# One table of numbers: the order of all steps, and the engines and queues of the movable ones, in a fused mLSTM and gated MLP kernel

## The chip, the cores and the metric

The kernel runs on one core of one Trainium2 chip, in one launch. The metric is the device time in microseconds; lower is better. The engines are named as in the profile: PE is TensorE (its weight loads are PEld), DVE is VectorE, ACT is ScalarE, POOL is GpSimd, SP is SyncE, which here only issues DMAs.

## The reference

The first half is a gated linear recurrence over 768 positions, for 4 batches and 8 heads of width 40; the second a gated MLP whose gate mixes positions.

```python
# q, k, v, o_gate: (4, 8, 768, 40); i_gate, f_gate: (4, 8, 768)
for t in range(S):
    m_new = np.maximum(f_gate[:, :, t] + m, i_gate[:, :, t])
    f_stab = np.exp(f_gate[:, :, t] + m - m_new)
    i_stab = np.exp(i_gate[:, :, t] - m_new)
    m = m_new
    C = f_stab[:, :, None, None] * C + i_stab[:, :, None, None] * np.einsum('bhd,bhe->bhde', vt, kt)
    n = f_stab[:, :, None] * n + i_stab[:, :, None] * kt
    h_tilde = np.einsum('bhde,bhe->bhd', C, qt)
    denom = np.maximum(np.abs(np.einsum('bhd,bhd->bh', n, qt)[:, :, None]), 1.0)
    y[:, :, t] = h_tilde / denom / (1.0 + np.exp(-o_gate[:, :, t]))
x = y.transpose(0, 2, 1, 3).reshape(B, S, H * D)        # (4, 768, 320)
h = np.maximum(x @ w_in, 0.0)                            # w_in (320, 1024)
u, v = h[..., :512], h[..., 512:]
v_n = (v - mean(v)) / np.sqrt(var(v) + 1e-06)
v_s = np.einsum('ts,bsd->btd', w_spatial, v_n) + b_spatial[None, :, None]
return (u * v_s) @ w_out                                 # w_out (512, 320)
```

## The kernel before

**Steps.** The program is a list of some 1,590 named steps. A step is a few instructions of one engine, or one DMA. It has a list of the engines that may run it, a few dependences, and a place in the table `ORDER` (lines 49 to 104). Nothing else sets the order: `ordered()` (line 162) reads the table from left to right, and the program emits the steps in that order. So the table gives each engine its queue, and each DMA queue (the one that SP issues, the one that ACT issues) its order. A name may carry a suffix: `:V`, `:A`, `:P`, `:S` puts the step on DVE, ACT, POOL or SP; without one it goes to the first engine of its list. The table also hands out the buffers: a tile takes the first free slot of its pool (`POOLS`, line 36) when its first step is reached, and gives it back behind its last step.

```python
    for t in order:
        for b in t.bufs:
            if b.slot is None:
                b.slot = open_[b.pool].pop(0)
            used[b] = used.get(b, 0) + 1
            if used[b] == b.users:
                open_[b.pool].append(b.slot)
```

So a load that is moved can land in another slot, and then waits for another tile's last reader. Pool QK (3 slots) holds the q and k of a chunk and, early on, the raw halves of w_in.

**The attention half.** The recurrence is done in 24 chunks n of 128 positions (6 for each batch, in the order of the batches), each of two halves of 64. First the gates are turned into the exponents g and a, in three pieces z of the sequence: positions 0 to 127, 128 to 383, 384 to 767 (`PIECES`). For piece z: loads f and i; on DVE or POOL the scan m, then fa, fs, the scan g, is, as; then gh, gl and ah, al, which split g and a into a high and a low float. Piece 0 of batch 0 goes directly into the tiles GM0 and AT0 (dg0 to dg3, da). The rest makes a round trip through DRAM: wg and wa write g and a (tiles gp and ap) to scratch (scr_g, scr_a; lines 391 and 395), gm (line 500) and ra (line 414) read them back as rows of the tiles GM and AT. ra01 and ra02 read pieces 1 and 2 of a for batch 0. Chunk 0 needs piece 0, chunks 1 and 2 piece 1, chunks 3 to 5 piece 2.

For chunk n on PE: s (line 518, 32 matmuls 64 columns wide: the scores), ex (line 521, one matmul 512 wide of AT and GM: the exponents), for batch 0 ebm (line 530, 512 wide), dc (lines 557 and 559, 16 matmuls: what the chunk adds to the state), pv (lines 585 and 586, 16 matmuls: the chunk's output), px (lines 618 and 619, three transposes of the output). Between them on ACT, DVE and POOL: W and Eb (exponentials of ex and ebm), ks (scores times W), q and kt (scaled q and k), d1, c1, d2, c2 (the state, from chunk to chunk), th (tanh of the output gate), den, xm, xg (the division and the gate), xh, xj, xl, xk (high and low halves of the transposed output).

**The MLP half.** Every fp32 product is three matmuls, of high and low halves (H·H, H·L, L·H). The weights are loaded raw and split: wi1j and wi0j for w_in (halves v and u, three row blocks j), ws for w_spatial, wo for w_out; of each _ld is the load (512 KB for one of w_in), _t, _b, _l are on DVE, _x on ACT, _h on either. For batch b, block k of 128 positions: V{b}{k} on PE (line 659, 8 matmuls 512 wide, x times w_in's half for v), then re, sq, va, po, nb, vn, vh, vl (relu, normalisation, split). pu (line 701) gives u. pb{b}{hf}{d}{s} (lines 711 to 713) mixes the positions, then g, gu, gh, gl; c (lines 734 to 736) multiplies by w_out, oc copies, out stores. The MLP steps of one batch stand among the attention steps of the next, so PE has both kinds until the last batch.

Of the kernel before, what the change touches and what calls it, by code (L numbers as in the profile page):

```python
# [49 lines left out]
mk1 i0 f0:A m0 rst0 ident ksz2 f1 rst1 rh0_1:A i1 fa0 qk0:A fs0 is0 wi10_ld ws02_ld g0 m1 as0 f2 gh0:V ah0 fa1 wi10_x al0 cg0 fs1 gl0 mk0 cg1 ca0 g1 ey0 gh1 i2:S wi12_ld  # L50
is1:P m2 wa0 rhz0 dg2 dg0:A as1 wi10_t da dg1 wi12_t ws02_h gl1 s0 dg3 wi00_ld:A ex0 rh0_0 fa2 ah1 fs2 ksz0:V g2 qz wg1 ksz1 cz0 al1:P wi10_b wa1 W0 wg0 wi12_x kt0:V rhz1
ebm0 ks0_1 wi11_ld wi00_t gm2 ra01 gm1 dc0 Eb0 rh1_1:A wi10_h eg21 is2:P q0_1 ks0_0 wi00_x as2:P th0 wi12_b c1_0 qk1 wi01_ld:A rhz2 gh2 eg00 pv0 ex1 wi12_h ey1 gl2:P
wi00_b wi10_l ah2 ws02_l:P wg2 ebm1 rh1_0:A wi11_t ebm2 wi12_l ex2 wi11_x wi02_ld:A Eb1 den0 wi11_b W1 xm0 al2:P d2_0:P xg0 kt1 wi11_h wi01_x wi01_t px0 c2_0 s1 rh2_1
qk2:A xj0:V xh0 wi11_l ws11_ld:A d1_1:P wa2 xl0 xk0 ks1_1 gm4:A q1_0 dc1 wi02_x ws12_ld wi01_b wi02_t Eb2 c1_1 q1_1 d2_1:P V00 rh2_0 wi01_h W2 q2_0 ks1_0 th1 gm3 wi00_h
wi02_b ra02 wi01_l pv1 q2_1 s2 rh3_0:A rh3_1:A ex3 c2_1 wi00_l den1 re00 qk3 xm1 ebm3 th2 sq00 kt2 ebm4 ks2_0 dc2 xg1 d1_2:P ks2_1 c1_2 s3 d2_2:P Eb3 px1 ex4 gm5:A W3
wi02_h Eb4 kt3 pv2 q3_1:V eg10 c2_2 xh1 ws01_ld:A qk4 ks3_0 d1_3:P ks3_1 th3 dc3 s4 q3_0 W4 den2 xm2 xg2 c1_3 eg20 xj1 qk5 s5 rh4_1 rh5_1:A eg11 xk1 pv3 d2_3 rh4_0 eg01
xl1 wo1_ld c2_3 ebm5 wi02_l ca1 Eb5 px2 rh5_0 ex5 xj2 ws00_ld:A den3 va00 xk2 ra12 W5 kt4 xm3 xh2 dc4 q4_0 V01 d1_4:P gm6 ks4_0 xl2 xg3 ws11_h ks4_1 px3 q5_1 c1_4 ws01_h
# [746 lines left out]
```

## Time and profile before

| | |
|---|---|
| three runs | 366.48, 367.25, 368.3 us (median 367.25) |
| the profiled execution, its own time | 365.34 us |
| its span, first to last instruction | 363.6 us |
| PE busy | 337.6 us, 93% of the span |
| DVE, ACT, POOL busy | 258.7, 126.9, 111.0 us |
| moved by DMA | 39.46 MB, 109 GB/s over the span |
| mean granted clock of TensorE | 0.972 |

The page cuts the span into 40 slices (9.1 us each), so slice 5 begins at 36 us. The granted clock is the share of TensorE's full speed that the throttle gave. A stretch (a view of the trace from one time to another) gives each engine's busy time within it, in the order PE, PEld, DVE, ACT, POOL, then the clock, the DMA engines' mean busy share and what they moved. The timeline gives one row for each instruction, with its start and length, and in brackets what it waited for. The chain of waits is followed back from the last instruction.

### The profile page before, as it was taken

To read this page: it belongs to the slowest core of one execution; us is meant where nothing else is said; L and a number is where in the kernel's file an instruction comes from. 1 tells how busy PE (TensorE), PEld (TensorE's weight loads), DVE (VectorE), ACT (ScalarE), POOL (GpSimd) and SP (SyncE) were. 2 spreads that over 40 slices of the span, in tenths; PEclk is the share of its full clock that TensorE was granted. 3 is DMA by queue.
4 is the path that set the end of the run, shared out by engine and by line. 5 is a ranking of instruction groups with operands and counts; after the bars stand their busy time and mean duration, and the time that the engine had idled before them with its cause. 6 is when DMAs were issued, how large, how long until landed. Compare 5 with 4: busy or idle time off the path is not lost.

```text
span 363.6 us, 9097 instructions
## 1 busy us (share of the span) xinstructions
PE 337.6 (93%) x3654; PEld 309.7 (85%) x3654; DVE 258.7 (71%) x590; ACT 126.9 (35%) x302; POOL 111.0 (31%) x133
## 2 busy tenths in 40 slices
PE   0378899999999899999999999999999999999995
PEld 0246697889999898999999988899999988999995
DVE  3989477997978848976498579766958686728152
ACT  1384426582324025272022253540310235432021
POOL 6475664686134241423100003332230231100000
PEclk9999657999999999999999999999999999999999
DMA  7489963843444770143405150443042300001002
GB/s 227 153 229 293 227 177 118 240 150 101 131 139 119 192 191 10 58 140 110 113 31 138 53 153 6 116 117 105 22 127 69 117 2 19 2 0 38 18 20 73
DMA packets 17218, 39.46 MB, mean 109 GB/s; under 512 B 4012, under 2 KB 7660, under 8 KB 17176
## 3 DMA queue, kind: packets, MB, share of 16 engines
q1 hardware_dynamic: 9540, 20.85, 20.7%
q10 hardware_dynamic: 7476, 17.92, 16.9%
q8 instruction: 29, 0.48, 0.6%
q0 software_dynamic: 160, 0.11, 0.1%
q14 instruction: 13, 0.11, 0.1%
HBM read 34.43 MB, written 4.42 MB: 107 GB/s over the span
## 4 chain that ended last, share of the span: by engine, by line
PE 79%; DMA 9%; DVE 6%; ACT 2%; issue 1%; SPq 1%; POOL 0%; DVEq 0%
PE pm L659 11%; PE pu L701 11%; PE pb L711 10%; PE pb L713 9%; PE pb L712 9%; PE s L518 5%; PE pv L585 4%; PE pc L734 4%; PE pc L736 3%; PE pc L735 3%; PE dc L557 3%; PE ex L521 2%; DMA AT<-scr_a 2%; DMA QK<-in_qk 2%; DMA scr_a<-ap 2%; PE px L618 2%
## 5 line engine op out<-in xcount | busy, mean ns | idle before, releaser
L711 PE MATMUL pb<-wsH,vH 128*128 128x384 f32 x192 | 66.5, 346 | 0.2 <-DVE vL L250 0.2
L713 PE MATMUL pb<-wsH,vL 128*128 128x384 f32 x192 | 64.8, 338 | 0.0
L712 PE MATMUL pb<-wsL,vH 128*128 128x384 f32 x192 | 64.8, 338 | 0.0
L250 POOL TENSOR_TENSOR KS<-QK,Eb 40x512 f32<-40x512 f32 x33 | 43.1, 1309 | 28.0 <-DMA Eb<-scr_e 18.1
L518 PE MATMUL s<-QK 40*64 40x64 f32 x768 | 30.3, 240 | 12.5 <-DMA QK<-in_qk 12.5
L518 PEld LDWEIGHTS s<-QK 40*64 40x64 f32 x768 | 27.7, 153 | 14.6 <-DMA QK<-in_qk 9.9
L711 PEld LDWEIGHTS pb<-wsH,vH 128*128 128x128 f32 x192 | 36.1, 188 | 1.4 <-DVE vL L250 0.5
L712 PEld LDWEIGHTS pb<-wsL,vH 128*128 128x128 f32 x192 | 36.1, 188 | 0.7
L671 POOL TENSOR_TENSOR st<-st,half_neg 128x1 f32<-128x1 f32 x24 | 13.5, 569 | 74.6 <-DVE st L669 63.9
L713 PEld LDWEIGHTS pb<-wsH,vL 128*128 128x128 f32 x192 | 36.0, 188 | 0.0
L250 DVE TENSOR_TENSOR pb<-pb,bsp 128x384 f32<-128x384 f32 x32 | 17.7, 561 | 24.3 <-PE pb L713 24.3
L250 DVE TENSOR_TENSOR KS<-s,W 64x512 f32<-64x512 f32 x48 | 32.7, 687 | 1.6 <-PE s L518 0.6
L701 PE MATMUL pu<-xH,wiH 128*128 128x384 f32 x96 | 32.6, 340 | 0.0
L701 PE MATMUL pu<-xH,wiL 128*128 128x384 f32 x96 | 32.4, 337 | 0.0
L734 PE MATMUL pc<-woH,gt 128*128 128x320 f32 x96 | 30.9, 322 | 0.0
L659 PE MATMUL pm<-wiH,xH 128*128 128x512 f32 x72 | 30.7, 426 | 0.2
L585 PEld LDWEIGHTS pv<-RH,KS 104*64 104x64 f32 x384 | 26.1, 148 | 5.2 <-issue 2.4
L533 ACT ACTIVATE W<-ex 128x512 f32<-128x512 f32 x24 | 14.3, 597 | 44.7 <-PE ex L521 35.0
L736 PE MATMUL pc<-woH,gt 128*128 128x320 f32 x96 | 29.8, 310 | 0.0
L585 PE MATMUL pv<-RH,KS 104*64 104x41 f32 x384 | 28.4, 240 | 1.4 <-DVE KS L250 0.9
L735 PE MATMUL pc<-woL,gt 128*128 128x320 f32 x96 | 29.6, 308 | 0.0
L659 PE MATMUL pm<-wiL,xH 128*128 128x512 f32 x72 | 29.1, 405 | 0.0
(159 smaller groups left out, 769.3 us busy)
## 6 DMA issues: line engine op xcount, KB each, us to landing
QK<-in_qk SPq DMA_DIRECT2D x15, 448.0 KB
RH<-in_vk ACTq DMA_DIRECT2D x24, 256.0 KB
RH<-in_vk SPq DMA_DIRECT2D x24, 256.0 KB
QK<-in_qk ACTq DMA_DIRECT2D x9, 448.0 KB
out<-o ACTq DMA_DIRECT2D x14, 160.0 KB
Eb<-scr_e SPq DMA_DIRECT2D x22, 80.0 KB
out<-o SPq DMA_DIRECT2D x10, 160.0 KB
wir<-in_w_in SPq DMA_DIRECT2D x3, 512.0 KB
```

Of the source, the lines that this page charges most:

```text
L250: return lambda e: e.tensor_tensor(out=out(), in0=in0(), in1=in1(), op=op)
L518: self.nc.tensor.matmul(o[64 - p0:128 - p0, h], q[p0:p0 + D, 0, h], q[p0:p0 + D, 1, h], start=True, stop=True)
L533: job(f"W{n}", act(512), lambda e: e.activation(out=self.T(W), in_=ext(), func=AF.Exp), r=[ex], w=[W], due=D0 + 1)
L585: self.nc.tensor.matmul(o[0:64, h], ks[0:ke, 0, h], v0[0:ke, h], start=True, stop=True)
L659: self.nc.tensor.matmul(pmt(), l, r, start=i == 0, stop=i == len(terms) - 1)
L701: self.nc.tensor.matmul(put(), w, x, start=i == 0, stop=i == len(terms) - 1)
L711: self.nc.tensor.matmul(pbt(), vH[:, cd], wh[:, s], start=s == 0, stop=False)
L712: self.nc.tensor.matmul(pbt(), vH[:, cd], wl[:, s], start=False, stop=False)
L713: self.nc.tensor.matmul(pbt(), vL[:, cd], wh[:, s], start=False, stop=s == NB - 1)
L734: self.nc.tensor.matmul(pct(), gH[:, c], wh[:, d], start=d == 0, stop=False)
L735: self.nc.tensor.matmul(pct(), gH[:, c], wl[:, d], start=False, stop=False)
L736: self.nc.tensor.matmul(pct(), gL[:, c], wh[:, d], start=False, stop=d == 3)
```

## The change

Only the table is another one. The diff is 54 lines of the table against 55, all of them different (later line numbers are one higher); one line of either:

```diff
 ORDER = """
...
-qk2:A xj0:V xh0 wi11_l ws11_ld:A d1_1:P wa2 xl0 xk0 ks1_1 gm4:A q1_0 dc1 wi02_x ws12_ld wi01_b wi02_t Eb2 c1_1 q1_1 d2_1:P V00 rh2_0 wi01_h W2 q2_0 ks1_0 th1 gm3 wi00_h
...
+ra11 d2_0:P s1 qk2 wa2:A c2_0 den0 ksz2 eg20 wi01_h q1_0 xm0 kt1 qk3:A wi02_x dc1 d1_1:P ey1 Eb2 xg0 ra02 px0 ex2 ebm3 ks1_1 c1_1 d2_1:P xh0 ks1_0 xj0 pv1 ws02_ld xk0
...
 """
```

The same steps stand in both tables. On other engines than before are: 59 DMAs that ACT issued and SP now issues, 49 the other way; 45 steps from DVE to ACT, 49 from ACT to DVE; 31 from DVE to POOL, 32 from POOL to DVE. PE's steps have one engine only; their order is another. In the first batch, from ex3 on, PE has

- before: ex3 ebm3 ebm4 dc2 s3 px1 ex4 pv2 dc3 s4 s5 pv3 ebm5 px2 ex5 dc4 V01 px3 V02
- after: ex3 s2 dc2 px1 s3 pv2 dc3 ebm4 s4 pv3 ex4 ebm5 px2 V01 ex5 px3 dc4 s5 V02

and ebm3 and pv1 stand ahead of ex3 in the second. The set of PE steps ahead of V02 is the same in both. Of PE's rows of narrow steps (s, dc, pv, ex, ebm, px, with no step of the MLP between them) the one between V00 and V01 is by far the longest in both orders; behind V02 none of either order sums to more than 3.6 us at full clock.

PE, just ahead of V01 (its tile is pm01). Before, V01 stands behind px2, ex5 and the 16 matmuls of dc4, of which the first is shown:

```order
L530 MATMUL eb5_654<-GM1_74,AT0_73 128x512
L618 MATMUL px2_660<-ident_71,x2_601 128x128 x2
L619 MATMUL px2_660<-ident_71,x2_601 64x128
L521 MATMUL ex5_665<-GM1_74,AT0_73 128x512
L557 MATMUL dc4_682<-RH1_80 40x41
```

In the changed kernel, the same place on PE, ahead of V01:

```order
L522 MATMUL ex4_627<-GM0_72,AT0_73 128x512
L531 MATMUL eb5_632<-GM1_74,AT0_73 128x512
L619 MATMUL px2_636<-ident_71,x2_603 128x128 x2
L620 MATMUL px2_636<-ident_71,x2_603 64x128
L660 MATMUL pm01_641<-wiH_83,xH00_389 128x512
```

V01 now directly follows px2; ex5, px3, dc4 and s5 stand between V01 and V02.

The queue of SP before, around wa2 (scr_a from ap2) and ra02 (AT0 from scr_a, 384 wide); RH2 from in_vk are the halves of chunk 2's v and k, wsr12 a third of half of w_spatial:

```order
L391 DMA scr_g_57<-gp2_257 32x12x64
L478 DMA RH2_81<-in_vk 64x1024
L395 DMA scr_a_59<-ap2_284 64x1x384
L453 DMA wsr12_382<-in_w_sp 128x768
L478 DMA RH2_81<-in_vk 64x1024
L500 DMA GM1_74<-scr_g_57 4x512
L414 DMA AT0_73<-scr_a_59 16x384
```

ACT in the changed kernel, around wa2; Eb1 and W1 are exponentials of chunk 1, ap2 by CAST is ah2, the step on RH0 is th0. Eight instructions ahead of this piece on ACT stands ra01 (AT0 from scr_a, 256 wide):

```order
L533 ACTIVATE Eb1_273<-eb1_266 128x512
L255 CAST ap2_279<-it_96 32x384
L396 DMA scr_a_59<-ap0_157 64x1x128
L479 DMA RH2_81<-in_vk 64x1024
L534 ACTIVATE W1_310<-ex1_286 128x512
L548 ACTIVATE RH0_79<-RH0_79 128x320
L396 DMA scr_a_59<-ap2_279 64x1x384
```

wa2 has moved from SP to ACT and stands there behind W1 and th0; ra02 is still issued by SP (behind qk2's load), ra01 by ACT instead of SP, and wa1 by SP in both (now behind the load of wi01).

## Rows read from the trace of the kernel before

**Rows 1.** The page: busy time of each engine, and TensorE's granted clock by slice.

```profile
PE 337.6 (93%) x3654; PEld 309.7 (85%) x3654; DVE 258.7 (71%) x590; ACT 126.9 (35%) x302; POOL 111.0 (31%) x133
...
PEclk9999657999999999999999999999999999999999
```

**Rows 2.** Stretches: from:to, us, busy PE PEld DVE ACT POOL, clock, DMA share, GB/s.

```profile
4.30:17.40 13.10, 2.27 (x33) 2.08 (x33) 11.01 (x24) 3.56 (x7) 6.94 (x12) 1.00 0.72 212
33.50:39.06 5.56, 2.31 (x65) 2.11 (x65) 4.74 (x12) 3.35 (x9) 2.77 (x3) 1.00 1.04 238
39.06:56.34 17.28, 17.28 (x269) 14.33 (x269) 10.02 (x24) 6.28 (x17) 10.49 (x13) 0.50 0.75 185
62.00:120.00 58.00, 57.96 (x736) 53.09 (x737) 51.00 (x119) 26.31 (x61) 28.77 (x28) 1.00 0.52 152
62.00:359.90 297.90, 296.29 (x3127) 277.30 (x3126) 214.64 (x496) 99.29 (x243) 73.65 (x82) 1.00 0.31 89
```

**Rows 3.** Stretches of one microsecond, the same columns.

```profile
59.00:60.00 1.00, 1.00 (x7) 0.75 (x5) 0.00 (x0) 0.00 (x0) 0.00 (x0) 0.73 0.62 213
```

**Rows 4.** The chain of waits from 24 to 60 us: start, length, what.

```profile
24.43 0.59 DVE wiL L250
...
25.16 1.00 POOL ap L250
26.17 6.03 DMA scr_a<-ap
32.21 6.71 DMA AT<-scr_a
39.06 0.76 PE ex L521
...
46.85 0.22 PE dc L557
...
48.10 3.21 PE s L518 x60
51.31 0.26 PE pv L585
...
53.18 0.72 PE eb L530
53.90 0.62 PE px L618 x2
...
54.73 0.43 PE ex L521
...
56.41 3.50 PE pm L659 x8
```

**Rows 5.** Timeline of PE: start, length, instruction.

```profile
30.72 0.79 PE L659 MATMUL pm<-wiH,xH 128*128 128x512 f32 x1
...
33.13 0.40 PE L659 MATMUL pm<-wiL,xH 128*128 128x512 f32 x1
...
59.99 0.48 PE L659 MATMUL pm<-wiH,xH 128*128 128x512 f32 x1
...
62.03 0.25 PE L585 MATMUL pv<-RH,KS 104*64 104x41 f32 x1
...
63.09 0.81 PE L557 MATMUL dc<-RH 64*40 64x41 f32 x16
...
75.03 1.15 PE L518 MATMUL s<-QK 40*64 40x64 f32 x32
```

**Rows 6.** Timelines of DVE, SP's queue and PE in the first 25 us.

```profile
4.32 0.41 DVE L340 TENSOR_TENSOR_SCAN mt<-ft,it 32x128 f32<-32x128 f32 x1 [4.32 <-DMA ft<-in_f_gate]
...
15.31 0.64 SPq L395 DMA_DIRECT2D scr_a<-ap  x1
...
19.92 0.31 SPq L414 DMA_DIRECT2D AT<-scr_a  x1
...
24.46 0.77 PE L521 MATMUL ex<-GM,AT 84*128 84x512 f32 x1 [0.15 <-ACT wi11w L429]
```

More of the change, by code (lines that the diff above doesn't have):

```diff
@@ L49 @@
 ORDER = """
-mk1 i0 f0:A m0 rst0 ident ksz2 f1 rst1 rh0_1:A i1 fa0 qk0:A fs0 is0 wi10_ld ws02_ld g0 m1 as0 f2 gh0:V ah0 fa1 wi10_x al0 cg0 fs1 gl0 mk0 cg1 ca0 g1 ey0 gh1 i2:S wi12_ld
-is1:P m2 wa0 rhz0 dg2 dg0:A as1 wi10_t da dg1 wi12_t ws02_h gl1 s0 dg3 wi00_ld:A ex0 rh0_0 fa2 ah1 fs2 ksz0:V g2 qz wg1 ksz1 cz0 al1:P wi10_b wa1 W0 wg0 wi12_x kt0:V rhz1
-ebm0 ks0_1 wi11_ld wi00_t gm2 ra01 gm1 dc0 Eb0 rh1_1:A wi10_h eg21 is2:P q0_1 ks0_0 wi00_x as2:P th0 wi12_b c1_0 qk1 wi01_ld:A rhz2 gh2 eg00 pv0 ex1 wi12_h ey1 gl2:P
@@ L53 @@
-wi00_b wi10_l ah2 ws02_l:P wg2 ebm1 rh1_0:A wi11_t ebm2 wi12_l ex2 wi11_x wi02_ld:A Eb1 den0 wi11_b W1 xm0 al2:P d2_0:P xg0 kt1 wi11_h wi01_x wi01_t px0 c2_0 s1 rh2_1
-qk2:A xj0:V xh0 wi11_l ws11_ld:A d1_1:P wa2 xl0 xk0 ks1_1 gm4:A q1_0 dc1 wi02_x ws12_ld wi01_b wi02_t Eb2 c1_1 q1_1 d2_1:P V00 rh2_0 wi01_h W2 q2_0 ks1_0 th1 gm3 wi00_h
-wi02_b ra02 wi01_l pv1 q2_1 s2 rh3_0:A rh3_1:A ex3 c2_1 wi00_l den1 re00 qk3 xm1 ebm3 th2 sq00 kt2 ebm4 ks2_0 dc2 xg1 d1_2:P ks2_1 c1_2 s3 d2_2:P Eb3 px1 ex4 gm5:A W3
@@ L56 @@
-wi02_h Eb4 kt3 pv2 q3_1:V eg10 c2_2 xh1 ws01_ld:A qk4 ks3_0 d1_3:P ks3_1 th3 dc3 s4 q3_0 W4 den2 xm2 xg2 c1_3 eg20 xj1 qk5 s5 rh4_1 rh5_1:A eg11 xk1 pv3 d2_3 rh4_0 eg01
-xl1 wo1_ld c2_3 ebm5 wi02_l ca1 Eb5 px2 rh5_0 ex5 xj2 ws00_ld:A den3 va00 xk2 ra12 W5 kt4 xm3 xh2 dc4 q4_0 V01 d1_4:P gm6 ks4_0 xl2 xg3 ws11_h ks4_1 px3 q5_1 c1_4 ws01_h
-xj3:V re01 ks5_1 wo1_x V02 gm7:A kt5:V half_neg q4_1 wo2_ld:A q5_0 xh3 pv4 d2_4 th4 c2_4 ks5_0 ws00_h th5 d1_5:P rh6_1 re02 dc5 ws00_l:P sq02 rh6_0:A we0 pu000 den4 xm4
@@ L101 @@
-c320 pu311 gl301 gh302 pb3125 gl302 c321 u310:V g312 c310 c311 pu312 c312 c313 oc31:V out31:A c300 pb3130 c301 u312 pb3100 c322 pb3101 pb3102 pb3103 pb3104 pb3105 g310
-gu310 gu312 c302 pu313 pb3110 pb3111 pb3112 pb3131 gh312 gh310 u313 gl310 pb3113 gl312 pb3114 u311 pb3115 pb3132 c323 pb3133 oc32 pb3134 g311 pb3135 gu311 gh311:V gl311
-out32:A g313 gu313 gh313 c303 c350 gl313 oc30 out30:A c351 c340 c352 c353 oc35 c341 out35:A c342 c343 oc34:V c330 out34 c331 c332 c333 oc33:V out33
+rhz0 rst0 qz i1:S mk0 rh2_1:A i0 rst1 f0 f1 m0 fa0 m1 fa1 f2 is1 wi10_ld:A fs0 cg0 fs1 wi00_ld ident half_neg i2:S g0 wi10_t wi12_ld g1 gh0 dg1 ca0 rh0_0:A wi10_x gl0
@@ new lines @@
+dg2:A as1 gh1:V is0:P m2 as0:P wi10_b ey0 wi11_ld fa2 dg3:A ah0 wi12_t rhz1 rh0_1:A wi12_x al0 gl1:P wg1 wi00_t cg1 ksz0 wi12_b wg0:A wi00_x rhz2 dg0 qk0:A wi11_x da
+wi11_t fs2:P g2 wi12_h ah1 ex0 wi01_ld gm1:A wi11_b W0 ebm0 al1:P wa1 ksz1:V eg21 gm2 rh1_0:A wi00_b wi12_l gh2 ra01:A eg10 is2:P s0 rh1_1:A wi01_x ks0_1 mk1 Eb0 wi10_h
+wi00_h:V kt0 eg01 cz0 wi11_h:V wi01_t dc0 ebm1 as2:P c1_0:A gl2:P wi00_l ks0_0 Eb1 wi10_l q0_1 qk1 ah2 wa0:A ebm2 wi01_b q1_1:V ex1 wg2 rh2_0:A wi02_ld pv0 gm3 W1 th0 al2
@@ new lines @@
+ra11 d2_0:P s1 qk2 wa2:A c2_0 den0 ksz2 eg20 wi01_h q1_0 xm0 kt1 qk3:A wi02_x dc1 d1_1:P ey1 Eb2 xg0 ra02 px0 ex2 ebm3 ks1_1 c1_1 d2_1:P xh0 ks1_0 xj0 pv1 ws02_ld xk0
+wi11_l rh3_1 xl0 wi02_t q2_1 th1 V00 c2_1 ex3 qk4:A s2 d1_2:P wi02_b den1 W2 Eb3 re00 sq00 wi01_l eg11 xm1 kt2:V q2_0 dc2 q3_0:V xg1 ks2_1 px1 W3 gm5:A s3 c1_2 ks2_0 xj1
+rh3_0 gm4 kt3 d2_2:P ws11_ld xk1 c2_2 pv2 wo1_ld:A eg00 dc3 xh1 ks3_1 den2 va00 d1_3:P c1_3 ks3_0 ebm4 we0:A s4 th2 wi02_h ws11_h xl1 xm2 q3_1 rh4_1 xg2 rh4_0 pv3 d2_3:P
@@ new lines @@
+th3 ws02_h ex4 Eb4 wi02_l ebm5 W4 px2 we1 V01 po00 ws11_l:P Eb5 rh5_0:A qk5 den3 c2_3 kt4 re01 xm3 xg3 ca1 rh5_1 xh2 ex5 px3 q4_0:V nb00 th4 dc4 gm6 ks4_0 d1_4:P xj2:V
+gm7 xl2 W5 s5 xk2 xj3 xh3 c1_4 wo1_t q4_1 d2_4:P ks4_1 V02 ws00_ld eb7_1:A sq01 kt5 c2_4 d1_5:P ks5_1 pv4 q5_1 rh6_1 wo1_x ra10 xk3 th5 ks5_0 qk6:A wo1_b xl3 dc5 den4
+va01 re02 q5_0 sq02 c1_5 va02 pu001 xm4 po01 wo1_h po02 rh6_0 wo1_l u001:V xg4 ws00_h ex6 W6 pv5 eb6_0:A px4 ex7 den5 wo2_ld vn00 xm5 W7 vh00 xg5 xh4 wo3_ld:A ws01_ld
@@ new lines @@
+pu000 px5 rh7_0:A V03 we2 vl00 xj5:V xj4:V nb02 xk5 xk4 xl4 gm8:A vn02 re03 wo2_t V04 vh02:V nb01 s6 kt6:V rh8_0 xh5:V xl5 V05 sq03 vn01 wo2_x va03 vh01 po03 ws01_h
+ws01_l:P ws00_l re04 vl02 nb03 ks6_0 pb0010 vl01 ws12_ld wo2_b sq04 va04 u000 ks6_1 po04 vn03 ra12:A dc6 wo2_h vh03 eb6_1:A q6_1:V re05 sq05 pu003 pb0011 c1_6 cz6 wo2_l
+nb04 vl03 pv6 th6 eb7_0:A qk7 ex8 W8 pb0000 pb0001 gm9 den6 d2_6:P rh7_1 xm6 pb0002 pb0030 pb0031 c2_6 s7 th7 bsp:A pb0003 vn04 ws02_l:P ws12_h u003 wo0_ld:A kt7 va05
@@ new lines @@
+px8 pb0112 pb0113 pb0114 c1_10 oc02 pb0130 pb0115 xj8:V xg9 xh8:V pb0101 xk8 ra21 q10_0:V ra31 xl8 rh11_0 d2_10:P eb11_0 c2_10 pb0131 px9 pb0102 pb0132 g011 th10 s10
+xj9:V u013:V s11 pb0133 rh12_0 rh12_1 q11_1 kt11 q11_0:V xk7 ks10_1 ks10_0 dc11 pv10 den10 pb0134 V10 th12 xh9 pb0135 gm12:A re10 xm10 d1_11:P ks11_1 qk12:A xg10 c1_11
+px10 ks11_0 gu011 g013 V12 pb0103 xh10 re12 gu013 out02:A out00 sq12 pb0104 pb0105 xl9 xk9 g010 va12 gu010 gh013 eb12_0 rh13_1 gh010:V gl010 po12 xj10 sq10 va10 po10
@@ new lines @@
+pb1122 ks15_0 th15 c1_15 xj13:V xk13 d2_15 pb1123 pb1130 c103 pb1124 xg14 oc10 ex17 gm18:A eb17_1 xh12 pb1131 xl12 px14 pb1132 c2_15 xh13 qk18:A q16_1:V d1_16:P rh17_0
+eb17_0 pb1125 pb1133 xk12 dc16 q16_0 xj14 xk14 rh17_1 W17 pv15 c1_16 xl13 den15 pv16 s17 den16 pb1101 xm15 pb1102 d2_16:P pb1103 th17 xm16 xg15 px15 xh15 g112 q17_1
+pb1104 xg16 xj15:V xh14:V xl14 xk15 gu112 gh112:V gl112 eb19_0 pu110 gm19 kt17 pb1105 c2_16 d1_17:P q17_0 px16 ks17_1 pb1134 V20 pb1135 u110 ks17_0 g110 xl15 re20 xj16
@@ new lines @@
+gl210 va31 px21 gu212 gh213:V pu301 gh212 po31 gl212 dc23 nb31 eb23_0 vn31:V gl213 vh31 xh21 pv22 out22:A s23 pu302 vl31 c230 c1_23 V32 q23_1:V den22 xm22 re32 c231
+u302:V ks23_0 out20:A sq32 c232 ks23_1 xg22 c233 c250 th23 va30 xl21 po30 nb30 oc23 vn30 xj21:V px22 xj22 xk22 xk21 out23 pv23 c240 c241 den23 c251 xh22 V33 c242 vh30
+re33 xm23 c252 xg23 c243 vl30 sq33 u301 xl22 px23 va32 xh23 c253 oc25 po32 nb32 pb3030 oc24 va33 V34 xl23 xj23 po33 xk23 out24:A out25 nb33 V35 pb3120 pb3000 pb3121
@@ L104 @@
+u312 c300 pb3100 pb3101 pb3102 c301 pb3103 pb3104 gu312 pb3110 pb3111 pb3112 pb3105 c302 g310 oc31:V gh312:V pb3113 pb3114 pb3115 g311 gu311 u310 gh311:V gl312 pb3130
+gu310 pb3131 pb3132 pb3133 pb3134 gh310 pb3135 out31 pu313 gl310 u313 gl311 c303 g313 gu313 oc30 gh313 c340 gl313 out30:A c341 c342 c330 c343 oc34:V c331 c332 out34 c350
+c333 c351 c352 oc33:V out33:A c353 oc35 out35:A
 """
```

72 lines of the change are left out of this document (30 added, 42 removed).

## The prediction

> **What bounds the kernel now.** I read the page first, then the stretches, the chain of waits, and the engines one by one. The page says TensorE: busy 93% of the span, and its granted clock sags only in slices 5 to 7 [rows 1]. The stretches make that sharper. From 62 us to the last matmul at 359.9 us PE is busy 296.3 of 297.9 us at full clock [rows 2]: there is 1.6 us to be had there, whatever the order. All the slack lies ahead of that, in the first batch's attention (chunks 0 to 5), where PE waits and then runs at half clock. Before 39.06 us it waits, 3.2 of the last 5.6 us [rows 2]; from 39.06 to 56.34 us it has no idle time, but the clock row reads 0.50, the lower of its two levels (1.2 GHz) [rows 2]. It comes back to 1.00 (2.4 GHz) at about 59.5 us [rows 3], 3 us after the step V01 began, whose matmuls are 512 columns wide [rows 4].
>
> So I measure by one mark: the start of V02, at 59.99 us [rows 5]. In both orders the same PE steps stand ahead of V02, and all PE work behind it is the same. If V02 comes d earlier and nothing behind it gets worse, the kernel is d shorter.
>
> The chain of waits names what holds V02: al2 on GpSimd at 25.16, the write of a's last piece to DRAM (wa2) 6.03 us, its reading back (ra02) 6.71 us, then ex3 at 39.06, and from there only PE work [rows 4].
>
> **The change, part by part.** No instruction is added or removed on PE. I take the PE row from ex3 to V02 at the half-clock prices of the chain [rows 4]: dc 1.2 (46.85 to 48.10), s 1.6 (two in 3.21), pv 1.87, eb 0.6 to 0.7, px 0.83, ex 0.43 (the first one 0.77), V01 3.5. Before: 39.06 + 17.3 = 56.4 = V01, which is what the trace has.
>
> *PE, after.* From ex3 to V01 now stand ex3 s2 dc2 px1 s3 pv2 dc3 ebm4 s4 pv3 ex4 ebm5 px2: 3 s, 2 dc, 2 pv, 2 px, 2 eb and 2 ex = 4.8 + 2.4 + 3.7 + 1.7 + 1.2 + 1.2 = 15.0 us at half clock. Behind V01 come ex5, px3, dc4 and s5, at full clock: s 1.15, dc 0.8 [rows 5], some 2.3 with ex and px. So V02 = ex3 + 15.0 + 3.5 + 2.3 = ex3 + 20.8. It breaks even with before at ex3 = 39.2, almost exactly where ex3 starts now. The question is therefore one: **when does ex3 start, and at which clock is the row behind it run?** At full clock the same row costs 1.15 x 3 + 0.8 x 2 + 1.06 x 2 [rows 5] and about 1.5 for px, eb and ex: 8.7 instead of 15.0.
>
> *The gate chain on VectorE.* m0 starts now at 4.32 [rows 6]. i0 now stands on ACT's queue behind rh2_1, 256 KB; at 238 GB/s [rows 2] that is 1.1, so m0 at 5.3. Up to 17.4 us DVE is 11.0 us busy [rows 2], of which two weight steps are 1.3, so the gate steps are 9.7; is0, as0, gl1, fs2 and ksz0 leave for GpSimd (-2.1, by their share of those 9.7), is1 and ksz1 come (+0.8): 8.4. Between m0 and al2 stand also 18 steps of 512 columns at 0.6 [rows 4]. Nine of them come before ks0_1: 5.3 + 8.4 + 5.4 = 19.1. There DVE now waits for s0, since qk0 is loaded into the buffer that wi12 leaves: I have that load issued at about 14.5 and s0 done at 21.4. Then nine steps: al2 at 27.0, against 25.16. In the page's terms this edit costs 1.9 us on the path to wa2, unless s0 is earlier.
>
> *The two round trips through DRAM.* Before, wa1 is issued at 15.31, ra01 at 19.92, ex1 starts at 24.46 [rows 6]: legs of at most 4.6 and 4.5 us. Now al1 stands on GpSimd behind ah1, which needs wg1 done, and wa1 on SP behind wi01's 512 KB: I put it at 17.3. ra01 now stands on ACT; queued behind it there are wi01's step, Eb0, Eb1, ah2 and W1, and DVE and PE wait for those. And wa2 moves from SP to ACT **behind W1**, which waits for ex1, which waits for ra01: the second round trip can't begin before the first has ended. With four legs of L each, and 1.6 for ex1, W1 and th0, ex3 = 17.3 + 1.6 + 4L, but not before 27.6 + 2L (al2). Two ends: the legs as short as 4.5 give 36.9; the four measured ones (at most 4.6 and 4.5, then 6.03 and 6.71 [rows 4, 6]) sum to 21.8 and give 40.7. I take 4.5 to 5: the two long ones ran at a DMA share of 1.04 [rows 2], and now ws02, ws12, qk4 and qk5 (1.6 MB) no longer stand among them.
>
> *V00.* The chain behind pv0 (den0, xm0, xg0, px0, then xk0, wi11_l, xl0 on DVE) starts after al2: 27.5 + 4.7 of DVE + 1.5 waiting for px0 = 33.7, so V00 at about 34.1 against 30.72 [rows 5], and it ends 2.8 later: 36.9. ebm3 and pv1 are now done before it. It is PE's last step before ex3, so ex3 is at 37 if ra02 has landed: no idle gap, where now there are 3.2 us. V00 is also what lifts the clock (0.77 us per matmul of 512 columns until then [rows 6], 1.00 in the clock row afterwards), and after it the clock lasted until 39.06, some 5.5 us after V00's end. From 37 on, that would cover 5.4 us of the row at full clock.
>
> *Sum.* ex3 at 37.0. At half clock throughout: V02 at 57.8, -2.2. With 5.4 us at full clock (of 8.7; the other 3.3 become 5.7): V02 at 53.9, -6.1. Data for s3, pv2, pv3 won't all be there on time (DVE is nearly full), so I take a value nearer the first: **-3.5 us**. The rest (59 DMA issues from ACT to SP, 49 back; 45 and 49 copies between DVE and ACT; 31 and 32 between DVE and GpSimd) lies beside PE's 296.3 busy us and moves the engines' sums by little; if that cover were gone, DVE, 51.0 of 58 us busy up to 120 us [rows 2], is late first. I give it 0 to +2. In the steady part no row of narrow steps (s, dc, pv, ex, px) is longer than 3.6 us in either order, so I expect no loss of clock there. The tail is the same: last c, one copy, one store.
>
> The Trainium skill, "TensorE: Matmul & The Clock Gate", section "Why this matters for your kernels", says that keeping TensorE continuously busy gets the full clock. The trace doesn't agree for this row: 17.28 us without idle time at 0.50 [rows 2]. By that rule the closed gap alone would keep the clock up; that is rival B.
>
> **The rivals.**
> A, the forecast: ex3 at 37 to 38, part of the row at full clock. -1.9 to -6: 361.2 to 365.3.
> B, the clock holds until V01: V02 = 37 + 8.7 + 1.9 + 2.3 = 49.9, -10; but the DVE has only 7 us of idle time up to 120 us [rows 2] to give, so -8: 359. For it: no gap before the row. Against: rows 2.
> C, what is won in the head is given back between 62 and 120 us, where DVE is at 88%, or the order shifts waits without removing any: within 1.8 us, 366.5. For it: DVE's sum there is the same in both orders.
> D, slower: the two round trips, now one behind the other on ACT, run at legs like 6.03 and 6.71. From a mean leg of 5.1 on, ex3 is past 39.2; at 5.7 it is at 41.7, V02 at 62.5, +2.5; at 6.4 (all four like the long ones) ex3 is at 44.5 and V02 at 65.3, +5.3, with PE idle before it. 370 to 372.5. For it: the DMA engines are full from 20 to 40 us now. Against: 1.6 MB less stands in the queues by then.
> That the change doesn't do what it says (the order as built differs) I give nothing: each engine's row is the table's.
>
> **How the numbers follow.** The profiled execution took 365.34 us (span 363.6), the median of the three runs is 367.25; I take the difference of 1.9 over unchanged. A: 367.25 - 3.5 = 363.7, chance 0.38. B 0.09. C 0.24. D 0.29. Half a per cent, 1.8 us, is about what a measurement can tell from no change. Faster: A and B, 0.47; same: C, 0.24; slower: D, 0.29. A's own range is 361 to 365.4. The range of 8 in 10 leaves out the half of B below 358.5 and the upper half of D with its ends: 358.5 to 371.
>
> **What would show it.** Right: ex3 (the fourth L522 exponent matmul of the first batch) at 36.5 to 38.5 with less than 1 us of PE idle before it; V01 directly behind px2; the clock row at 1.00 until past 40; the start of V02 between 54 and 58; PE idle under 3 us from V02 on. Wrong: DVE waiting much longer than 2.3 us at ks0_1 (then qk0 is the fault); ACT idle for several us at ra01 or wa2 (D); a clock that falls in the steady part; PE waits on DVE between 62 and 120 us (C).

## The result, and the profile after

| | before | after |
|---|---|---|
| median of the runs, us | 367.77 (366.48 to 369.61, 4 runs) | 356.50 (355.25 to 357.15, 4 runs) |
| profiled execution, us (span) | 365.34 (363.6) | 357.15 (355.4) |
| mean granted clock | 0.972 | 0.998 |
| start of ex3 / V01 / V02, us | 39.06 / 56.34 / 59.99 | 38.95 / 48.22 / 52.42 |
| TensorE idle from V02 to its last matmul, us | 1.6 | 1.0 |

The changed kernel takes 0.9686 of the time before, 95% interval 0.9634 to 0.9737: 11.3 us less by the medians, 8.2 us less by the two profiled executions. Every ratio here goes by the fast runs alone (a run over 1.5% above the fastest of its kernel is left out); medians and ranges hold every run. The forecast was 363.7 (358.5 to 371). The direction was right, the size was not.

The page of the changed kernel, busy time and TensorE's granted clock by slice:

```profile
PE 330.2 (93%) x3654; PEld 303.6 (85%) x3654; DVE 259.0 (73%) x595; ACT 125.7 (35%) x298; POOL 106.1 (30%) x132
...
PEclk9999999999999999999999999999999999999999
```

Beside [rows 1]: the slices 5 to 7 that read 6, 5 and 7 now read 9, and TensorE's busy time is 7.4 us less for the same 3,654 matmuls. They are not fewer, they run faster.

Stretches of the changed kernel (us, busy PE PEld DVE ACT POOL, clock, DMA share, GB/s): V00; from ex3 to V01; from V01 to V02; from V02 to the last matmul:

```profile
35.24:38.95 3.71, 3.71 (x9) 2.74 (x9) 3.54 (x9) 1.09 (x2) 2.03 (x2) 1.00 1.06 235
38.95:48.22 9.27, 9.24 (x234) 7.58 (x234) 7.58 (x20) 6.91 (x17) 6.00 (x7) 1.00 0.78 192
48.22:52.42 4.20, 4.20 (x80) 3.49 (x77) 3.93 (x10) 2.53 (x8) 4.05 (x5) 1.00 0.67 166
52.42:351.70 299.28, 298.28 (x3136) 278.68 (x3134) 218.41 (x506) 99.72 (x241) 71.51 (x82) 1.00 0.33 93
```

The second line answers the 17.28 us at 0.50 of [rows 2]. ex3 starts at the same time in both kernels, 0.1 us apart; the row of narrow steps behind it takes 9.3 us at 1.00 instead of 17.3 us at 0.50. The two rows are not quite the same work: before's has one ex, one ebm and one dc more, 2.3 us at the prediction's half-clock prices. V02 is 7.6 us earlier, and of the 8.2 us between the two profiles only 0.6 us is left for everything behind it.

The chain of waits of the changed kernel, from DVE's division for chunk 0 to ex3 (start, us, what):

```profile
30.08 0.51 DVE pv L251
...
30.69 0.50 DVE x L604
...
31.23 0.69 PE px L619 x2
...
35.24 3.71 PE pm L660 x8
38.95 0.43 PE ex L522
```

In [rows 4] ex3 is released by a DMA (ra02). Here it is released by V00, the step ahead of it on TensorE. V00 stands 4.5 us later than before (30.72 in [rows 5]) and its end is ex3's start, so there is no wait between the wide step and the narrow row. The queues of ACT and SP in the changed kernel (ra01, wa2, ra02):

```profile
20.68 0.33 ACTq L415 DMA_DIRECT2D AT<-scr_a  x1
...
28.91 0.60 ACTq L396 DMA_DIRECT2D scr_a<-ap  x1
...
31.74 0.30 SPq L415 DMA_DIRECT2D AT<-scr_a  x1
```

wa2's leg is 2.8 us (28.91 to 31.74) against 6.03 before, so the later write costs nothing.

### The profile page after: what moved, and what is told of

It reads as the page before. It is cut to its first block, busy times and chain, and to the rows that moved or that the text cites. A ratio compares the mean times of both kernels' runs of the same rounds, so it can differ in the third digit from the quotient of the medians.

```text
span 355.4 us, 9097 instructions
## 1 busy us (share of the span) xinstructions
PE 330.2 (93%) x3654; PEld 303.6 (85%) x3654; DVE 259.0 (73%) x595; ACT 125.7 (35%) x298; POOL 106.1 (30%) x132
## 4 chain that ended last, share of the span: by engine, by line
PE 84%; DVE 7%; DMA 4%; ACT 2%; issue 1%; ACTq 1%; DVEq 0%
PE pm L660 12%; PE pu L702 12%; PE pb L712 10%; PE pb L714 9%; PE pb L713 9%; PE s L519 6%; PE pv L586 5%; PE pc L735 4%; PE pc L737 4%; PE pc L736 4%; PE dc L558 3%; DMA wir<-in_w_in 2%; DMA QK<-in_qk 2%; DVE KS L251 2%; PE ex L522 1%; PE px L619 1%
## 5 line engine op out<-in xcount | busy, mean ns | idle before, releaser
L251 POOL TENSOR_TENSOR KS<-QK,Eb 40x512 f32<-40x512 f32 x25 | 32.0, 1281 | 26.4 <-DMA QK<-in_qk 15.3
L519 PE MATMUL s<-QK 40*64 40x64 f32 x768 | 28.6, 229 | 1.7 <-DMA QK<-in_qk 1.7
L519 PEld LDWEIGHTS s<-QK 40*64 40x64 f32 x768 | 25.7, 143 | 5.0 <-DMA QK<-in_qk 2.2
L522 PE MATMUL ex<-GM,AT 84*128 84x512 f32 x24 | 11.2, 473 | 18.6 <-DMA AT<-ap 17.0
```

The costliest lines, as they stand in the source:

```text
L251: return lambda e: e.tensor_tensor(out=out(), in0=in0(), in1=in1(), op=op)
L519: self.nc.tensor.matmul(o[64 - p0:128 - p0, h], q[p0:p0 + D, 0, h], q[p0:p0 + D, 1, h], start=True, stop=True)
L522: self.nc.tensor.matmul(ext(), AT.t[:, k * 128:(k + 1) * 128], GM.t, start=True, stop=True)
```

## The experiments

Theory W: in the kernel before, the waits behind V00 (TensorE idle for 3.2 of 5.5 us) cost the clock, and the whole narrow row is then run at half of it; the new order leaves no wait there. Rival R: it is not the wait but the narrow row itself, which is longer in the table of before, with V01 behind it all. Rivals H and S: what lies ahead of V02 and what lies behind it. Theory Q, formed after the first four kernels: a second wait, ahead of s11, does the same at 122 us in most runs of before.

### A wait put back into the changed kernel

```diff
 on SP's queue
-ra02 ws02_ld rh3_1 rh3_0 gm4 ws11_ld rh4_1
+ws02_ld rh3_1 rh3_0 gm4 ws11_ld rh4_1 ra02
```

> The changed table with one move: ra02 (the reading back of a's last piece) stands on SP's queue behind ws02_ld, rh3, gm4, ws11_ld and the first half of rh4, so ex3 waits for it behind V00 as it does in before. Theory W: TensorE waits 3 to 6 us between V00's end (about 39) and ex3 (42 to 45), the clock falls to 0.50 within or behind that wait, the narrow row takes about 15 us, V02 at 61 to 66, time 365 to 370. Rival R: the clock holds at 1.00, and the time grows by the wait alone, V02 at 55.5 to 58.5, time 359.5 to 362.5.

No other queue changes. Measured: 369.09 us (368.11 to 370.51), ratio 1.0017 (0.9984 to 1.0050). All of the gain is gone, and all of W's figures are met. ex3 in TensorE's timeline (start, us, instruction, and in brackets the wait and what ended it):

```profile
43.21 0.76 PE L522 MATMUL ex<-GM,AT 84*128 84x512 f32 x1 [5.58 <-DMA AT<-scr_a]
```

The stretches of that wait and of the narrow row up to V01:

```profile
37.60:43.21 5.61, 0.04 (x1) 0.03 (x1) 1.56 (x3) 1.66 (x5) 0.00 (x0) 0.72 0.58 157
43.21:58.84 15.63, 15.63 (x235) 12.91 (x235) 8.36 (x22) 5.80 (x12) 7.07 (x8) 0.50 0.24 73
```

The clock falls inside the wait, and the same narrow row that took 9.3 us takes 15.6 without an idle moment. ex3 is 4.3 us later than in the changed kernel, V02 (65.35) 12.9 us: 4.3 us of the wait's price is the wait, the other 8.6 the clock. Rival R is out: row and place of V01 are those of the changed kernel. That the time equals that of before is partly chance: V02 is 5.4 us later than there, and behind V02 this execution takes 302.6 us, as the changed kernel does (303.0).

### The waits filled in the kernel before

```diff
+    def fill(self, tile, j, count):
+        w = self.F("wiH").t
+        for _ in range(count):
+            self.nc.tensor.matmul(tile, w[:, j, DH:DH + 128], w[:, j, DH:DFF], start=True, stop=True)
...
 s2:
+8 x fill, into the bank that s2 then writes
 ex3:
+6 x fill, into the bank that ex3 then writes
```

> The order of before, untouched; TensorE's two waits behind V00 are filled with matmuls of weights whose result is overwritten (8 of 512 columns ahead of s2, 6 ahead of ex3, into the banks that s2 and ex3 then write). Work is added, none is taken away or moved. Theory W: clock 1.00 from 33 us on, ex3 at about 39.1 to 39.5, V01 at 48 to 49, V02 at 51 to 53, time 358 to 361. Rival R: the clock falls to 0.50 at 39 to 41 as before, time 367 to 369. Rival D (the gain of the changed order lies in DVE's and the DMAs' order): no gain, 366 to 369.

Measured: 362.94 us (361.15 to 365.00), ratio 0.9852 (0.9787 to 0.9917). 14 matmuls of work more, and the kernel is faster. The stretch from ex3 to V01, in the order of before:

```profile
41.30:53.66 12.36, 10.39 (x270) 8.44 (x269) 8.69 (x23) 5.47 (x15) 7.06 (x9) 1.00 1.04 214
```

The clock row reads 1.00 where [rows 2] has 0.50. This is before's own row, with V01 behind it, so rival R fails here too. W's times were missed: V02 starts at 55.86, 4.1 us earlier, and not 7 to 9. ex3 now starts at 41.35, behind the fillers, against 39.06, and TensorE, now faster, waits 2.0 us in the row, 1.28 of them for a load of q and k; none of these waits lost the clock. So what the waits behind V00 cost was the clock, and an order made for a slow row gives a part back in new waits. Behind V02 this kernel takes 3.3 us more than the profiled one of before (306.9 against 303.6 us); s11 waits 1.67 us in it, and the clock reads 0.50 behind that, which led to theory Q.

### One swap in the kernel before

```diff
 on PE
-V00 pv1 s2 ex3
+pv1 V00 s2 ex3
```

> The order of before, with one swap on TensorE: V00 (8 matmuls 512 wide) stands behind pv1 instead of ahead of it, so that V00 ends where s2 and ex3 begin and no wait lies between V00 and the narrow row. Theory W (the waits behind V00, 3.2 us of the 5.5 us up to ex3, are what costs the clock; the order after V00 costs nothing): V00 ends near 39, the clock stays at 1.00 through the narrow row, which then takes about 9 us instead of 17.3, V02 starts at 51.5 to 54 instead of 60, and the time is 359 to 362 against 367. Rival R (the narrow row of before, longer and without V01 inside it, is what costs the clock): the clock reads 0.50 again from about 5 us behind V00 on, V02 at 58 to 62, time 365 to 369.

Measured: 367.53 us, the median of ten (361.44 to 369.71; before 369.05 beside it), ratio 0.9891 (0.9832 to 0.9949). The median is in R's range and not in W's. Two waits in TensorE's timeline of the profiled execution (367.25 us), of pv1 and of pv3, the second ended by nothing that the profile shows:

```profile
35.28 0.30 PE L585 MATMUL pv<-RH,KS 104*64 104x41 f32 x1 [3.07 <-DVE KS L250]
...
51.86 0.20 PE L586 MATMUL pv<-RH,KS 128*64 128x41 f32 x1 [1.84 <-issue]
```

The stretches from s2 to pv3's wait, that wait, and behind it:

```profile
40.18:50.00 9.82, 9.58 (x259) 8.13 (x259) 7.59 (x17) 6.02 (x17) 5.54 (x8) 1.00 0.95 219
50.00:52.11 2.11, 0.27 (x7) 0.20 (x5) 1.39 (x3) 0.00 (x0) 1.96 (x3) 1.00 1.05 265
52.11:54.69 2.58, 2.58 (x42) 1.82 (x38) 1.66 (x7) 1.84 (x5) 1.81 (x3) 0.67 0.43 83
```

The swap does what W says for over ten microseconds: full clock from s2 on, where R has it fall some 5 us behind V00. But it put V00 behind pv1's own wait (3.07 us), and the clock is lost behind a second wait, in pv3, at the end of the row. V02 at 57.66, between W's 51.5 to 54 and R's 58 to 62: W's numbers were too good, since moving one step opens waits elsewhere. One run of the ten has a mean clock of 1.00, and it took 361.44 us, within W's 359 to 362.

### The head of one, the rest of the other

```diff
 h_ab
+the changed table as far as V02, then what is left, in the order and on the engines of before
 h_ba
+the table of before as far as V02, then what is left, in the order and on the engines of the changed one
```

> The changed table up to V02, and all that is left from there in the order and on the engines of before. Theory H (all of the gain lies ahead of V02): V02 at 52 to 53, time within 1.5 us of the changed kernel, 355.5 to 358. Rival S (a part of the gain lies behind V02, in the order of the steady stretch): 359 to 363.

> The order of before up to V02, and all that is left from there in the order and on the engines of the changed kernel: the other half. Theory W with Q: ex3 at 39, clock 0.50 from there to V01, V02 at 59 to 61 as before; no wait ahead of s11 and no second stretch at half clock; ratio to before 0.985 to 0.995. If the order behind V02 were worth nothing: 0.997 to 1.003. If the head were worth less than the marks say: below 0.98.

Measured: h_ab 361.33 us (359.58 to 362.99), ratio 0.9806 (0.9742 to 0.9870). V02 at 51.97, as in the changed kernel, but 4.8 us more in the end, outside H's range and within S's. Part of it is s11, in TensorE's timeline:

```profile
117.30 0.97 PE L519 MATMUL s<-QK 40*64 40x64 f32 x13 [1.47 <-DMA QK<-in_qk]
```

The stretch behind it:

```profile
118.00:124.00 6.00, 6.00 (x40) 5.75 (x38) 2.78 (x8) 0.00 (x0) 2.12 (x3) 0.50 0.96 240
```

Here the clock is lost a second time, in the middle of the steady stretch, 1.47 us of wait and then over 6 us at half pace. It is not all: one of the four runs has a mean clock of 1.00 and still took 360.21 us. [rows 2] show 1.6 us of idle time behind 62 us in the kernel before. Most of that is the same wait, in its timeline:

```profile
122.96 1.15 PE L518 MATMUL s<-QK 40*64 40x64 f32 x32 [1.03 <-DMA QK<-in_qk]
```

In that execution it cost no clock: s11 takes 1.15 us, the full pace.

h_ba took 370.99, 372.56 and 375.35 us, and once 427.86 at a mean clock of 0.756, which was not followed up; its ratio of 1.0172 (1.0065 to 1.0278) is outside all expectations. At the seam pv4 waits for POOL, in TensorE's timeline:

```profile
66.60 0.25 PE L586 MATMUL pv<-RH,KS 128*64 128x41 f32 x1 [2.81 <-POOL KS L250]
```

and the clock goes again in the stretch behind it:

```profile
66.60:80.00 13.40, 12.90 (x116) 11.40 (x117) 9.79 (x31) 7.80 (x18) 4.55 (x6) 0.75 0.49 140
```

It says nothing on what the rest of the new table is worth, only that the two halves of a table don't come apart freely.

### The second wait

```diff
-... s9 s8 qk13:A ... kt11 qk11 pv10 s11 ...
+... s9 s8 qk11:A ... kt11 qk13 pv10 s11 ...
```

b_qk is the kernel before with this exchange of two loads, h_ab_qk is h_ab with it, and b_again is the kernel before for another profile.

> The order of before, in which two loads change places: q and k of chunk 11 (s11 waits 1.03 us for them at 122 us in the profile of before, 1.5 to 1.7 us in the three kernels that got there sooner, and behind it they show a clock of 0.50 for some 4 us) are loaded where those of chunk 13 were, and those of chunk 13 where chunk 11's were. The head is untouched. Theory Q (that wait and the half clock behind it are in most runs of before, though not in its profiled one, and are the part of the gain that the head does not explain): no wait ahead of s11, clock 1.00 from 60 us on, ratio to before 0.985 to 0.993, runs within 363 to 366. Rival (the rest of the gain is DVE's order behind V02): ratio 0.997 or more.

> The changed table up to V02, the order of before behind it, and the same exchange of the loads of chunks 11 and 13. Theory Q with W: the clock is 1.00 from 39 us on, the dip at 117 to 124 us is gone, ratio to before 0.968 to 0.974, 356 to 359: what is left to the changed kernel is the waits of 2.0 us between 55 and 62 us. Rival (DVE's order behind V02 carries the rest): the ratio stays at 0.978 to 0.982.

> The kernel before once more, for another profile of it. Its runs spread over 364 to 371 us, its profiled one is among the fastest. Theory Q: a run of 367 to 370 shows, beside the half clock from 39 us on, a second stretch at half clock behind the wait of s11 at 120 to 126 us, which the first profile lacks. Rival: it shows the same clock row and the time goes elsewhere.

Measured: b_again took 368.94 us. Its V02 starts at 60.06, 0.1 us from the first profile of the same kernel, though the waits behind V00 are smaller: 1.45 us in all up to ex3, not 3.2. s2 and ex3 in TensorE's timeline:

```profile
37.72 1.15 PE L518 MATMUL s<-QK 40*64 40x64 f32 x32 [0.42 <-DMA QK<-in_qk]
...
39.71 0.47 PE L521 MATMUL ex<-GM,AT 84*128 84x512 f32 x1 [0.84 <-DMA AT<-scr_a]
```

ex3 itself still runs at the full pace here (0.47 us, against 0.76), and the clock falls some 2 us later: it reads 0.87 from 41 to 42 us and 0.50 from 42 to 43. Then s11:

```profile
123.53 1.89 PE L518 MATMUL s<-QK 40*64 40x64 f32 x32 [1.58 <-DMA QK<-in_qk]
```

and the stretches from that wait on:

```profile
122.00:128.00 6.00, 4.47 (x41) 4.25 (x42) 4.82 (x12) 0.00 (x0) 1.54 (x2) 0.64 0.64 144
128.00:132.00 4.00, 4.00 (x18) 4.00 (x18) 0.76 (x3) 0.00 (x0) 2.80 (x4) 0.69 0.55 167
```

That is the stretch that the first profile lacks. From V02 to the end it takes 307.1 us (367.2 - 60.1), the first took 303.6: 3.5 us, nearly all of the 3.6 between the two executions. b_qk has no wait there: 363.58 us (360.59 to 366.38), ratio 0.9888 (0.9788 to 0.9989), as Q has it, though its interval nearly reaches no change. Its head shows something more. The row behind ex3 is at half clock as before, but the full clock comes back within it (stretches from ex3 to V01):

```profile
39.73:50.50 10.77, 10.77 (x189) 9.02 (x191) 6.36 (x14) 4.33 (x12) 6.80 (x9) 0.54 0.95 230
50.50:53.83 3.33, 3.33 (x85) 2.68 (x81) 2.82 (x10) 1.14 (x3) 2.69 (x3) 1.00 0.76 175
```

The exchanged loads are issued 50 us later and can't have done that. V02 starts at 56.04, so b_qk's profile has a gain that isn't the exchange's, and what the exchange alone is worth is known only roughly. The kernel before has such executions too. The runs of it beside the experiments list mean clocks from 0.961 to 0.981; the five fastest of these 37, 364.07 to 365.34 us, are the ones at 0.981. The first profile lost the clock in the head alone and has 0.972, so in those five the loss in the head was shorter.

h_ab_qk: 358.95 us (357.85 to 360.48), ratio 0.9792 (0.9717 to 0.9868). The time is within what Q expected, the ratio is not; the ratio's interval is as wide as the question. Its clock is 1.00 throughout, and what is left to the changed kernel (2.5 us by the medians) stands in two waits behind V02:

```profile
51.92:62.00 10.08, 8.28 (x106) 6.69 (x105) 8.67 (x22) 4.69 (x12) 9.01 (x8) 1.00 0.89 243
62.00:130.00 68.00, 67.83 (x848) 63.11 (x847) 56.77 (x129) 25.46 (x59) 27.87 (x30) 1.00 0.61 158
```

1.8 us of idle time before 62 us, 0.2 in the 68 us behind it. In the changed kernel the stretch from 52.42 to the last matmul has 1.0 us in all. The two waits are 0.94 us ahead of a dc, ended by an earlier pv of TensorE itself, and 0.84 us ahead of a pv, ended by DVE. So some 2 us of the gain lie in the order behind V02, which in the changed table is ready for an early TensorE; which steps of it do that was not taken apart.

### Both losses taken from the kernel before

b_fill_qk is b_fill with the exchange of the two loads; a_again is the changed kernel beside it.

> The order of before with both clock losses taken away and nothing else: the 14 filling matmuls ahead of s2 and ex3, and the loads of q and k of chunks 11 and 13 exchanged. Theory W with Q: clock 1.00 from V00 to the end, V02 at 53 to 56, ratio to before 0.973 to 0.982, 358.5 to 361.5. If the changed kernel's gain needed its own order of DVE and DMAs for more than some 3 us: ratio above 0.985.

> The changed kernel once more, beside the others of this call: 0.964 to 0.973 of before, its runs within 2 us of each other, its clock row without a stretch at 0.50 (theory W: nothing in it waits behind V00 long enough to lose the clock).

Measured side by side: before 367.89 us, b_fill_qk 361.23 (359.50 to 366.30), ratio 0.9843 (0.9765 to 0.9921); a_again 356.87 (355.39 to 359.73), ratio 0.9724 (0.9663 to 0.9784). The first is within W with Q by its time; its ratio lies just above the range, and the interval covers it. Two of its six runs, 364.88 and 366.30 us, list a mean clock of 0.981 and so lost it after all; the other four took 359.50 to 361.25. The changed kernel's ratio is at the upper end of its range, and its runs lie 4.3 us apart, not within 2. Its clock row has no stretch at 0.50, and its TensorE timeline shows the full pace sooner than the first profile did (px0, the last matmul of V00, ex3):

```profile
31.04 0.44 PE L619 MATMUL px<-ident,x 128*128 128x128 f32 x2 [0.35 <-DVE x L604]
...
35.76 0.39 PE L660 MATMUL pm<-wiL,xH 128*128 128x512 f32 x1
35.99 0.39 PE L522 MATMUL ex<-GM,AT 84*128 84x512 f32 x1
```

The row behind ex3 has three waits here, of 0.25 to 0.63 us, and holds the clock through 10.9 us up to V01. Its V02 starts at 51.10. Stretches of b_fill_qk behind V01 and around s11:

```profile
53.39:70.00 16.61, 16.12 (x145) 13.08 (x143) 15.62 (x46) 11.92 (x29) 9.63 (x10) 1.00 0.73 200
110.00:130.00 20.00, 20.00 (x306) 18.97 (x301) 14.88 (x36) 4.20 (x9) 6.59 (x8) 1.00 0.77 199
```

Full clock and no wait at 122 us in this execution. With its steps in their old order, and only the two losses of clock removed, the kernel has 6.7 of the 11.0 us. The other 4.4 us: V02 starts at 55.66 against 52.42 and 51.10 in the two profiles of the changed kernel, so 3.2 to 4.6 us are in the head, and from V02 to the end the three take the same, 302.9, 303.0 and 303.1 us. In the head the fillers and the waits of the old order hold ex3 back (42.4, against 38.95 and 35.99); how much each of them takes wasn't measured.

### V01's place

```diff
 on PE
-px2 V01 ex5 px3 dc4 s5 V02
+px2 ex5 px3 dc4 V01 s5 V02
```

> The changed order with V01 moved on TensorE from behind px2 to behind dc4 (ex5, px3 and dc4 now stand ahead of it, as ex5 and dc4 do in before): the narrow row between V00 and V01 is 10.8 us long at full clock instead of 9.3, with no wait put in. Theory W: the clock holds at 1.00 through the longer row, V02 moves by less than 1 us, ratio to before 0.966 to 0.973. Rival R (the length of the narrow row decides): the clock falls ahead of V01, V02 at 54 to 57, ratio 0.975 to 0.985.

Measured: 361.56 us (359.05 to 363.01), ratio 0.9838 (0.9742 to 0.9933), V02 at 58.18. Rival R's numbers were hit or passed, for another reason, px3's wait in TensorE's timeline:

```profile
50.24 0.66 PE L619 MATMUL px<-ident,x 128*128 128x128 f32 x2 [1.41 <-DVE x L604]
```

The stretches from ex3 on, cut before and behind that wait:

```profile
39.12:48.40 9.28, 9.25 (x236) 7.40 (x234) 7.73 (x21) 6.94 (x17) 5.82 (x7) 1.00 0.79 200
48.40:52.30 3.90, 2.49 (x39) 1.75 (x37) 3.02 (x7) 0.43 (x1) 3.75 (x5) 0.69 0.87 218
52.30:58.18 5.88, 5.16 (x43) 3.82 (x41) 1.02 (x4) 2.06 (x7) 0.46 (x1) 0.63 0.50 117
```

The row of 9.3 us is at 1.00 as before the move. Then px3, which V01 no longer covers, waits 1.41 us for DVE, and the clock goes within that wait. The condition of the expectation (no wait put in) wasn't met, so the run doesn't test the length of the row. What it does show is what V01's place does: it gives TensorE 2 us of work while DVE makes x3.

### A faster version, tried

```diff
 the changed kernel, wide filling matmuls whose results are overwritten:
+4 ahead of s0, 5 ahead of ex1, 6 ahead of px0
```

> The changed order, untouched, with 15 matmuls of 512 columns put into TensorE's waits of the first 31 us (4 ahead of s0, 5 ahead of ex1, 6 ahead of px0), whose results are overwritten: a version meant to be faster than both. In the changed kernel's trace all matmuls up to 38.9 us run at half pace (0.76 to 0.80 us for 512 columns, V00 3.7 us). Theory W (work without waits brings the full pace): V00 takes 2.1 us, starts at 34.4 when DVE's xl0 is done, ex3 at 36.5 if ra02 has landed and 38.5 at the latest, V02 0.5 to 2.4 us sooner than in the changed kernel, ratio to before 0.962 to 0.968. Rival (the fillers only delay s0 and ex1, which other engines wait for): V00 no sooner, ratio 0.969 to 0.975.

Measured: 358.50 us (357.75 to 359.68), ratio 0.9757 (0.9705 to 0.9809), against 356.87 for the changed kernel beside it: not faster. The medians differ by 1.6 us, less than the 4.3 us between the changed kernel's own runs. The stretch from s0 to pv0:

```profile
19.42:29.69 10.27, 7.95 (x77) 5.59 (x76) 6.11 (x10) 4.09 (x10) 6.97 (x9) 0.87 0.71 187
```

ex1 starts at 29.14 instead of 25.57 us. The fillers stand ahead of steps that ACT and DVE wait for, and the clock row shows 0.87 in a stretch where the changed kernel's reads 1.00. V00 does run at full pace, but only from 36.29 us on, later than without them. The time is the rival's or worse, not W's.

## Why the prediction was wrong

- **What bounds the kernel, and the mark.** Right for the profiled pair: 7.6 of 8.2 us are the start of V02. The premise that 1.6 us is all there is to be had behind 62 us failed. It was read from one execution; in b_again the 1.03 us wait of [rows 2]'s 1.6 us had become 1.58 us and cost 3.5 us with the clock. The sentence that takes the difference of 1.9 us between profile and median over unchanged rests on the same premise: most runs of before have more half clock than the profiled one, and the changed order has no such wait. The 3.1 us between 11.3 and 8.2 have the size of that loss; in the runs without a profile it was not seen directly.
- **The price of the row.** Right: 8.7 us at full clock and 15.0 at half were given for ex3 to px2; the changed kernel took 9.3, and a_gap, the same row at half clock, 15.6.
- **ex3 at 37.** It was 38.95, and 35.99 in the second profile. So in the first pair none of the 7.6 us comes from an earlier ex3, of which the forecast had made 2. DVE waited 3.5 us for s0, not 2.3, and al2 began at 28.3; V00 started at 35.2 and took 3.7 us, not 2.8, since the pace rose only at its end. In the second profile it had risen by px0 (31.04), and V00 took 2.1. The legs through DRAM were shorter than the 4.5 to 5 taken: at most 3.5 us for wa1 (17.23 to ra01 at 20.68), 2.8 for wa2, and in the second profile at most 4.3 for ra02 (31.66 to ex3 at 35.99). So in these two profiles the sum of four legs, and with it rival D, did not set ex3.
- **How long the clock lasts: the step that failed.** The sum gave the clock 5.4 us behind V00's end, because it had lasted that long in [rows 2], and then took a value near no gain at all. In [rows 2] TensorE was idle for 3.2 of those 5.5 us; the 5.5 us end in those waits and don't say how long the clock would last without them. With the waits gone it lasted through all 9.3 us and on. Rival B said so and had a chance of 0.09. That its price of -8 lies so near the measured -7.6 is luck in part: its V02 was 49.9 against 52.42, its ex3 2 us too early, and the cut from -10 to -8 was for DVE's idle time, which did not bind. The argument against it was a row without idle time at 0.50, but that row begins behind a wait: it shows that such a row need not bring the clock back, not that it takes it away.

  The rule of the Trainium skill that stood beside it ("TensorE: Matmul & The Clock Gate", section "Why this matters for your kernels"), that a continuously busy TensorE gets the full clock, agrees with the runs for keeping the clock and not for getting it back: the changed kernel's row held 1.00 for 9.3 us, and in a_gap the same row, 15.6 us without idle time, stayed at 0.50.
- **The steady part.** "No narrow row longer than 3.6 us in either order, so no loss of clock there" asked the wrong question: the loss at 122 us comes behind a wait for a load, not from a long row. Rival C did not happen: from 62 to 120 us the changed kernel's TensorE has no idle time at all (58.00 of 58.00 us). An early TensorE does meet waits where the old order follows, 1.8 us in h_ab_qk, but between 55 and 60 us, and only one of the two is ended by DVE.

## What to carry to other kernels

Where one engine bounds the kernel and its clock follows its work, a wait of one or two microseconds must be priced with the clock of the stretch behind it: here, with ex3 at the same time in both kernels, V02 came 7.6 us later behind 3.2 us of waits. Look for what ended the work before a slow stretch, not only at the stretch. Another step in the place of the wait kept the clock (V01 ahead of px3), and so did work whose result is thrown away (b_fill); in a_warm, where other engines waited for the step behind it, such work gained nothing. And take two profiles of a kernel whose runs spread: 3.5 of the 3.6 us between the two of this kernel were one wait and the slow stretch behind it.

## What the runs showed of the hardware

- The clock row of the records reads 1.00 from the start, while the matmuls run at half pace: in the changed kernel's first profile a matmul of 512 columns takes 0.63 to 0.80 us, and V00 starts one every 0.43 us, up to V00's end; in V01 they take 0.39 to 0.48 us and start every 0.23. In these traces a half clock at the start is seen in the length of a matmul, not in that row.
- The same row of narrow steps, without idle time, got its full clock back within 10.8 us in b_qk, and in the first profile of before not in 17.3 us, but 3 us into V01. What decides this was not found.
- Waits of nearly one size went either way: 1.03 us ahead of s11 left the clock at 1.00, 1.47 and 1.58 us in the same place took it. Behind V00, 1.45 us in several waits were enough in b_again; in a_again 1.4 us in several waits within the row were not. This is one source of the spread between one kernel's runs (364 to 371 us), and the time that the half clock lasts in the head, different in b_qk's profile, is another.
- A small transfer through DRAM took 2.8 us or 6.0 (wa2), and ra02 3.3 us in a_gap (issued at 39.91, ex3 at 43.21) against 6.7 before. What stood ahead of them in the queues differs; that this is the reason was not tested.
